# Loading q and k two rows at a time, turned by DMA transposes and sorted by copies, in a fused attention and feed-forward kernel

## The chip, the cores and the metric

The kernel runs on one core of a Trainium2 chip. The metric is the time of one execution on the device in microseconds (us). The kernel before takes 318.61 us, the median of 3 runs (318.08 to 319.79).

## The reference

What is computed is an attention over a sliding window of 64 positions, whose output feeds a two-layer network with the activation h cos h:

```python
batch, n_heads, seq, head_dim = (8, 8, 576, 64)
scores = scale * np.matmul(q, k.transpose(0, 1, 3, 2))
mask = (rel >= 0) & (rel < window)            # rel = pos[:, None] - pos[None, :], window = 64
scores = np.where(mask, scores, -1000000000.0)
attn = np.exp(scores - np.max(scores, axis=-1, keepdims=True))
attn = attn / (np.sum(attn, axis=-1, keepdims=True) + 1e-09)
x = np.matmul(attn, v)                        # to rows (batch, seq) x columns (head, dim): 4608 x 512
h = x @ w_in                                  # w_in: 512 x 2048
out = (h * np.cos(h)) @ w_out                 # w_out: 2048 x 512
```

All inputs and the output are float32. The kernel computes in bf16 with float32 sums.

## The kernel before

**The row tiles.** The outer loop runs over 9 tiles of 512 rows (`mt`, 0 to 8). Each has two halves. In the first, for each of 16 blocks `ff` of 128 hidden columns, four matmuls of 512 columns (`h_ps`, line 341) are summed in PSUM; ScalarE (ACT) takes the sine of h + pi/2 (line 486) and VectorE (DVE) multiplies it with h to `gT` (line 489). In the second half 64 matmuls (`out_ps`, line 501) multiply `gT` with w_out. The h_ps blocks use five PSUM banks in turn (`H_BANKS`), so that the matmuls of a block need the bank that an earlier block's gT has freed.

**The attention lies between them.** While tile `mt` is worked on, the scores of batch `mt` + 1 are computed in between, for the outputs that tile `mt` + 1 needs. Heads go in pairs (`PAIRS` = 4): a pair's 2 x 64 dimensions fill the 128 partitions. Keys must lie as kT (dimensions of a pair on partitions, positions along the free axis). For batches 2 to 7 queries lie in `qB` (`qblocks`), one block for each 64 positions, where a pair's two heads stand in a diagonal of two 64 x 64 squares with zeros beside them, so that one matmul (line 248) computes both heads. A group of three or four such units goes through scores on TensorE (PE), mask and maximum on DVE (line 268), exp on ACT (line 279), the inverse of the sum on DVE (line 286), the multiplication to `w` on GpSimd (POOL, line 293), and a DMA transpose from the SP queue to `wT` (line 305). The products with v (`values`, line 320) close the tile.

**How q and k of batches 2 to 7 come.** `load_chunk` (line 146) loads 96 positions of all 8 heads, with a cast to bf16, from POOL's queue: 6 chunks each of q and k, 64 elements to a row of a head. Queries are turned by PE: `transposed` (line 180) makes six transposes of 96 x 128 for a pair into one PSUM tile, and `put_block` copies the two heads on DVE into their places in `qB` (line 113, the shared copy helper). Keys of batch 2 go the same way (`tr_k`, `put_k`, the copy on ACT), those of batches 3 to 7 by `turn_k` (line 213): six DMA transposes a batch from SP, each of four 128-column blocks, straight into kT. Batches 0 and 1 are loaded in another form (`load_heads`, nine consecutive rows to a partition) and turned by PE, line 177.

**The order.** Every engine works through its own queue in order; the kernel writes that order by hand. Tile 0 follows the list `FIRST`. After that `at(time, fn, ...)` puts steps on a plan, and `pump(time)` issues those that are due after each block of matmuls. A tile is 32 units of this plan, of which the first 16 follow the blocks `ff` and the others four out_ps matmuls each; the times are no microseconds, they only fix the places in the queues. Scores begin at unit 14.6 of a tile (line 382). The last group of a batch has its inverse, its w and its wT at the tile's end (line 386). DMA loads are issued by POOL, DMA transposes and stores of the output by SP, so a waiting instruction there holds up the transfers behind it. Loads of v (line 152, five a batch) come at the head of a tile; `spread_v` copies half of v on POOL (line 113) before the scores.

Of the kernel before, what the change touches and what calls it, by code (L numbers as in the profile page):

```python
# [15 lines left out]
BF16 = mybir.dt.bfloat16  # L16
# [7 lines left out]
NU = 9  # L24
NC, NP = 6, 96
# [33 lines left out]
def kernel(  # L59
# [28 lines left out]
    qtiles = [const.tile([128, S], BF16, name=f"qT{i}") for i in range(2 * PAIRS)]  # L88
    qblocks = [const.tile([128, NU, 2, 64], BF16, name=f"qB{i}") for i in range(2 * PAIRS)]
# [42 lines left out]
    def rows_tile(name):  # L132
        return ld.tile([128, NC * H * D], BF16, tag=name, name=name)
# [36 lines left out]
    def transposed(name, b, p):  # L170
        t_ps = ps_t.tile([128, S], BF16, tag="t", name=f"t{name}_ps")
        of = st[name, b]
        if b < 2:
            for c in range(RC):
                for h in range(2):
                    d = slice(64 * h, 64 * h + 64)
                    nc.tensor.transpose(t_ps[d, 64 * c:64 * c + 64], of[d, p, 64 * c:64 * c + 64], ident[d, d])  # L177
        else:
            for c in range(NC):
                nc.tensor.transpose(t_ps[:, NP * c:NP * c + NP], of[:, c, 128 * p:128 * p + 128], ident[:NP, :NP])  # L180
        return t_ps


    def in_order(t_ps, to, b):
        return (t_ps.rearrange("d (c p) -> d p c", c=RC), to.rearrange("d (p c) -> d p c", c=RC)) if b < 2 else (t_ps, to)
# [4 lines left out]
    def put_q(b, p, engine=None):  # L190
        of, to = in_order(st.pop(("tq", b, p)), qtiles[b * PAIRS + p], b)
        if b:
            copy(engine, to, of)
        elif engine == "a":
            nc.scalar.mul(to, of, scale)
        else:
            nc.vector.tensor_scalar(to, of, scale, None, ALU.mult)

    def put_block(b, p, h):
        d = slice(64 * h, 64 * h + 64)  # L200
        copy("d", qblocks[(b % 2) * PAIRS + p][d, :, h], st["tq", b, p][d].rearrange("d (j t) -> d j t", j=NU))
# [10 lines left out]
    def turn_k(b, c):  # L212
        nc.sync.dma_start(out=k_tile(b)[:, :, c * NP:c * NP + NP], in_=st["k", b][:, c], transpose=True)

    def put_k(b, p, engine="a"):
        kt = k_tile(b)[:, p]
        of, to = in_order(st.pop(("tk", b, p)), kt, b)
        copy(engine, to, of)
# [13 lines left out]
    def g_scores(n, which):  # L232
# [8 lines left out]
        for u, (b, p, j) in enumerate(units):  # L241
# [5 lines left out]
            if b > 1:  # L247
                nc.tensor.matmul(out=s_ps[:, u].rearrange("p (a t) -> p a t", a=2),  # L248
                                 lhsT=qblocks[(b % 2) * PAIRS + p][:, j].rearrange("d h t -> d (h t)"), rhs=rhs,
                                 start=True, stop=True, skip_group_check=True)  # L250
                continue
            for h in range(2):
                d = slice(64 * h, 64 * h + 64)
                nc.tensor.matmul(out=s_ps[d, u].rearrange("p (a t) -> p a t", a=2),  # L254
                                 lhsT=qtiles[b * PAIRS + p][d, 64 * j:64 * j + 64], rhs=rhs[d], start=n >= n_first,
                                 stop=n >= n_first or u == len(units) - 1, skip_group_check=True)
# [91 lines left out]
    def clear(i):  # L348
        nc.gpsimd.memset(qblocks[i].rearrange("d j h t -> d (j h t)"), 0.0)
# [18 lines left out]
    def at(time, fn, *args):  # L368
        plan.append((time, len(plan), fn, args))
# [25 lines left out]
    for b in range(1, B):  # L395
        t0 = T * (b - 1)
        for p in range(PAIRS):
            t_q = 7 + 1.8 * p if b == 1 else t0 + 1 + 2.5 * p if b == 2 else t0 + 1 + 3.5 * p
            steps = (((0, tr_q), (0.01, tr_k), (0.02, put_q), (0.03, put_k)) if b == 1 else
                     ((0, tr_q), (0.02, put_block, 0), (0.5, put_block, 1)) +  # L400
                     (((9.5 - 0.8 * p, tr_k), (9.51 - 0.8 * p, put_k)) if b == 2 else ()))
            for lag, fn, *args in steps:
                at(t_q + lag, fn, b, p, *args)
        if b > 1:
            for c in range(NC):
# [10 lines left out]
    for p in range(PAIRS):  # L416
        at(T + 3 + 4 * p, clear, PAIRS + p)
# [13 lines left out]
    for t in qblocks[:PAIRS]:  # L431
        nc.vector.memset(t.rearrange("d j h t -> d (j h t)"), 0.0)
# [108 lines left out]
```

## Time and profile before

| | |
|---|---|
| median of 3 runs | 318.61 us (318.08 to 319.79) |
| span of the profiled execution | 316.6 us |
| instructions in the profile | 7858 |
| busy: PE, DVE, ACT, POOL | 300.1, 227.8, 238.3, 196.6 us |
| DMA | 39.91 MB in 150697 packets, 139392 of them under 512 B |
| queue of POOL's loads (q0) | 99824 packets, 18.36 MB |
| queue of SP's transposes and stores (q1) | 50688 packets, 20.85 MB |

The runs were timed without the profiler; the profiled execution's own time is known by its span, from its first instruction to its last, and the median lies 2.0 us above it for what surrounds the span. PE stands for TensorE's matmuls and PEld for its weight loads, which overlap them. In a list of instructions "out<-in" names the tiles, then come the shapes (partitions x elements), the number of instructions and their time; a bracket at the end gives the idle time of the engine before and what ended it. L113 is the helper `copy`, so copies are told apart by their tiles. SPq and POOLq are the queues in which DMAs are issued: the time of such a row is that of issuing, not of the transfer. In a table of windows each engine's entry is its busy time and, in brackets, its number of instructions; the last three numbers are the granted clock of TensorE, the share of the DMA engines and GB/s.

The stages' length hardly varies in the middle: the windows 160 to 192, 192 to 224 and 224 to 256 us have PE busy for 31.76 us each, with a granted clock of 1.00.

### The profile page before, as it was taken

To read this page: it belongs to the slowest core of one execution; us is meant where nothing else is said; L and a number is where in the kernel's file an instruction comes from. 1 tells how busy PE (TensorE), PEld (TensorE's weight loads), DVE (VectorE), ACT (ScalarE), POOL (GpSimd) and SP (SyncE) were. 2 spreads that over 40 slices of the span, in tenths; PEclk is the share of its full clock that TensorE was granted. 3 is DMA by queue.
4 is the path that set the end of the run, shared out by engine and by line. 5 is a ranking of instruction groups with operands and counts; after the bars stand their busy time and mean duration, and the time that the engine had idled before them with its cause. 6 is when DMAs were issued, how large, how long until landed. Compare 5 with 4: busy or idle time off the path is not lost.

```text
span 316.6 us, 7858 instructions
## 1 busy us (share of the span) xinstructions
PE 300.1 (95%) x2580; PEld 157.5 (50%) x2620; DVE 227.8 (72%) x871; ACT 238.3 (75%) x789; POOL 196.6 (62%) x228
## 2 busy tenths in 40 slices
PE   3678999999999999999999999999999999999995
PEld 2544545555555544545554555555555554454443
DVE  5976778689767977697859885997599758335801
ACT  3978689868998689869986998699868996115600
POOL 8896156799969767897788878986832630000000
PEclk9979999999999999999999999999999999999999
DMA  6999996699959994899989997999692442011011
GB/s 97 170 211 207 207 148 90 70 194 162 160 92 98 151 228 85 88 153 231 124 91 140 230 123 83 158 218 127 77 179 92 81 105 100 2 66 69 0 66 66
DMA packets 150697, 39.91 MB, mean 126 GB/s; under 512 B 139392, under 2 KB 146176, under 8 KB 150656
## 3 DMA queue, kind: packets, MB, share of 16 engines
q0 software_dynamic: 99824, 18.36, 75.7%
q1 hardware_dynamic: 50688, 20.85, 32.5%
q8 instruction: 20, 0.33, 0.4%
q14 instruction: 21, 0.17, 0.2%
q10 hardware_dynamic: 144, 0.20, 0.2%
HBM read 36.70 MB, written 9.44 MB: 146 GB/s over the span
## 4 chain that ended last, share of the span: by engine, by line
PE 81%; DVE 6%; ACT 5%; POOL 3%; issue 2%; DMA 2%; POOLq 0%
PE h_ps L341 35%; PE out_ps L501 34%; ACT e L279 3%; PE s_ps L248 3%; DVE gT L489 3%; PE o_ps L320 3%; DMA k<-in_k_dram 2%; PE tq_ps L180 2%; PE s_ps L254 1%; POOL w L293 1%; PE out_ps L356 1%; DVE qB L113 1%; PE tw_ps L302 1%; POOL v L113 1%; PE tk_ps L177 1%
## 5 line engine op out<-in xcount | busy, mean ns | idle before, releaser
L341 PE MATMUL h_ps<-xT,w_in 128*128 128x512 bf16 x556 | 130.5, 379 | 2.9 <-ACT xT L113 1.0
L501 PE MATMUL out_ps<-w_out,gT 128*128 128x512 bf16 x543 | 130.9, 379 | 1.2 <-issue 0.5
L486 ACT ACTIVATE sin<-h_ps 128x512 f32<-128x512 f32 x144 | 83.6, 598 | 39.2 <-PE h_ps L341 36.2
L489 DVE TENSOR_TENSOR gT<-h_ps,sin 128x512 bf16<-128x512 f32 x144 | 92.2, 685 | 27.1 <-ACT sin L486 26.2
L279 ACT ACTIVATE e<-s,negm 128x128 f32<-128x128 f32 x256 | 98.7, 388 | 1.0 <-DVE negm L268 0.9
L293 POOL TENSOR_TENSOR w<-e,rden 128x512 bf16<-128x512 f32 (+1 forms) x78 | 74.0, 958 | 35.6 <-DVE rden L286 29.1
L341 PEld LDWEIGHTS <-w_in 128*128 128x128 bf16 x576 | 54.3, 98 | 60.7 <-issue 2.4
L501 PEld LDWEIGHTS <-gT 128*128 128x128 bf16 x560 | 51.5, 98 | 49.7
L268 DVE CUSTOM_DVE_ANT_0 s<-s_ps,mask 128x128 f32<-128x128 f32 x256 | 58.2, 285 | 1.9 <-PE s_ps L254 1.6
L279 ACT ACTIVATION_READ_ACCUMULATOR e<-s,negm 128x1 f32 x256 | 48.1, 188 | 0.0
L146 POOL DMA_DIRECT2D q<-in_q_dram x36 | 28.9, 804 | 12.3 <-PE h_ps L341 4.7
L152 POOL DMA_DIRECT2D v<-in_v_dram x40 | 34.1, 874 | 3.0 <-DMA k<-in_k_dram 2.0
L146 POOL DMA_DIRECT2D k<-in_k_dram x36 | 29.0, 806 | 3.2 <-DMA k<-in_k_dram 2.4
L113 ACT COPY out_sb<-out_ps 128x512 f32<-128x512 f32 (+1 forms) x18 | 10.1, 563 | 25.7 <-PE out_ps L501 20.2
L286 DVE RECIPROCAL rden<-den 128x4 f32<-128x4 f32 (+1 forms) x80 | 13.9, 173 | 20.9 <-ACT e L279 18.3
L113 DVE CAST xT<-o_ps 128x512 bf16<-128x512 f32 x27 | 17.5, 678 | 9.9 <-PE o_ps L320 9.9
L113 DVE COPY out_sb<-out_ps 128x512 f32<-128x512 f32 x18 | 12.4, 689 | 16.6 <-PE out_ps L501 12.6
L248 PEld LDWEIGHTS <-qB 128*128 128x128 bf16 x216 | 17.0, 98 | 14.6 <-DVE negm L268 0.6
L113 POOL COPY v<-v 64x2048 bf16<-64x2048 bf16 (+1 forms) x11 | 18.7, 1701 | 5.4 <-DMA v<-in_v_dram 5.0
L248 PE MATMUL s_ps<-kT,qB 128*128 128x128 bf16 x216 | 21.9, 219 | 0.2 <-DVE negm L268 0.2
L113 DVE COPY qB<-tq_ps 64x576 bf16<-64x576 bf16 x48 | 21.6, 450 | 0.3
L268 DVE DVE_READ_ACCUMULATOR2_ANT negm<- 128x1 f32 x256 | 21.3, 83 | 0.0
(57 smaller groups left out, 187.5 us busy)
## 6 DMA issues: line engine op xcount, KB each, us to landing
out_dram<-out_sb SPq DMA_DIRECT2D x16, 512.0 KB, 6.8
v<-in_v_dram POOLq DMA_DIRECT2D x32, 128.0 KB, 6.2
q<-in_q_dram POOLq DMA_DIRECT2D x36, 96.0 KB, 7.1
k<-in_k_dram POOLq DMA_DIRECT2D x36, 96.0 KB, 7.5
w_out<-in_moe_w_out_dram POOLq DMA_DIRECT2D x2, 1024.0 KB, 16.4
w_in<-in_moe_w_in_dram POOLq DMA_DIRECT2D x2, 768.0 KB, 11.8
wT<-w SPq DMA_TRANSPOSE x66, 2.9
out_dram<-out_sb SPq DMA_DIRECT2D x3, 256.0 KB, 2.0
```

What stands on the lines that cost most here:

```text
L113: {"a": nc.scalar.copy, "p": nc.gpsimd.tensor_copy}.get(engine, nc.vector.tensor_copy)(out, in_)
L146: nc.gpsimd.dma_start(out=st[name, b][:, c].rearrange("p (h d) -> p h d", h=H), in_=src.rearrange("h p d -> p h d"))
L152: nc.gpsimd.dma_start(out=vt.rearrange("p (h d) -> p h d", h=H), in_=v[b, :, c * 128:c * 128 + n, :].rearrange("h p d -> p h d"))
L248: nc.tensor.matmul(out=s_ps[:, u].rearrange("p (a t) -> p a t", a=2), lhsT=qblocks[(b % 2) * PAIRS + p][:, j].rearrange("d h t -> d (h t)" ...
L268: nc.vector.tensor_tensor_reduce(out=s[:, u], in0=s_ps[:, u], in1=mask[:, 2 - j % 2 if j else 0], scale=-scale if b else -1.0, scalar=BIG, ...
L279: nc.scalar.activation(e[:, u], s[:, u], AF.Exp, bias=negm[:, u:u + 1], scale=1.0 if n < n_first else -1.0, accum_out=den[:, u:u + 1])
L286: nc.vector.reciprocal(out=rden[:, 0:len(groups[n])], in_=den[:, 0:len(groups[n])])
L293: (nc.gpsimd if engine == "p" else nc.vector).tensor_tensor(out=w[:, 0:u], in0=e[:, 0:u], op=ALU.mult, in1=rden[:, 0:u].unsqueeze(2).to_br ...
L341: nc.tensor.matmul(out=st["h", ff], lhsT=w_in_sb[:, ks, ff * 128:ff * 128 + 128], rhs=st["xT", mt][:, ks], start=start, stop=stop)
L486: nc.scalar.activation(sin, h_ps, AF.Sin, bias=math.pi / 2.0)
L489: nc.vector.tensor_tensor(out=gt[:, e], in0=h_ps, in1=sin, op=ALU.mult)
L501: nc.tensor.matmul(out=o_ps[e], lhsT=gT[ff // 2][:, ff % 2, ms * 128:ms * 128 + 128], rhs=w_out_sb[:, ff], start=ff == 0, stop=ff == n_ff - 1)
```

## The change

It concerns q and k of batches 2 to 7.

- `load_rows` takes the place of `load_chunk`. A partition gets two consecutive rows of a head (128 elements), and a batch's q or k comes in two DMAs of four heads each (96 x 12 x 128), in place of six: four loads a batch from POOL, not twelve.
- `turn` sends each half through one DMA transpose from SP (12 blocks of 96 x 128). Its result X has the even rows' dimensions on partitions 0 to 63 and the odd rows' on 64 to 127. There are four such DMA transposes a batch, placed at units 0.3 to 2.3 of the tile in which the batch's scores are computed; the PE transposes of q and of k of batch 2, `put_block` and the former `turn_k` go.
- `sort_rows` copies X into kT and into qB, every second position at a time: four copies for k and four for q, each of 64 partitions x 1152 elements, two of each four on DVE and two on POOL, at units 6.2 to 11.7 of the same tile. Both halves of X must have landed for each.
- X shares its two buffers with the tiles that hold the queries of batches 0 and 1. `qB` becomes one tile for each parity of batches. `clear` still zeroes the second one's four parts on POOL in tile 1.

The program's order after the change has on PE 168 transposes fewer with their weight loads. On SP a tile (2 to 6) has: the last wT of the old one, Xk, a store, Xk, a store, Xq, Xq, then the new wT. On POOL: the last w, five loads of v, a sort of k, a load of k, a sort of k, two loads (k, q), a sort of q, a load of q, a sort of q, then `spread_v` and the w. On DVE the sorts of k stand before and after the ninth gT of the tile (ff = 8), those of q before and after the thirteenth (ff = 12). The first score matmul of a tile waits for DVE and POOL. In tile 1 the four X transposes come one after the other, and the memsets of `clear` stand between POOL's loads and sorts.

```diff
-NC, NP = 6, 96
+NG, NP = 3, 96
...
-    qtiles = [const.tile([128, S], BF16, name=f"qT{i}") for i in range(2 * PAIRS)]
-    qblocks = [const.tile([128, NU, 2, 64], BF16, name=f"qB{i}") for i in range(2 * PAIRS)]
+    qblocks = [const.tile([128, PAIRS, NU, 2, 64], BF16, name=f"qB{i}") for i in range(2)]
...
-    def load_chunk(name, b, c):
+    def load_rows(name, b, half):
         if (name, b) not in st:
-            st[name, b] = rows_tile(name)[0:NP].rearrange("p (c x) -> p c x", c=NC)
-        src = {"q": q, "k": k}[name][b, :, c * NP:c * NP + NP]
-        nc.gpsimd.dma_start(out=st[name, b][:, c].rearrange("p (h d) -> p h d", h=H),
-                            in_=src.rearrange("h p d -> p h d"))
+            st[name, b] = rows_tile(name)[0:NP].rearrange("p (m x) -> p m x", x=2 * D)
+        m = slice(half * H // 2 * NG, (half + 1) * H // 2 * NG)
+        src = {"q": q, "k": k}[name][b].rearrange("h (g p c) d -> p (h g) (c d)", g=NG, c=2)
+        nc.gpsimd.dma_start(out=st[name, b][:, m], in_=src[:, m])
...
-    def put_block(b, p, h):
-        d = slice(64 * h, 64 * h + 64)
-        copy("d", qblocks[(b % 2) * PAIRS + p][d, :, h], st["tq", b, p][d].rearrange("d (j t) -> d j t", j=NU))
...
-    def turn_k(b, c):
-        nc.sync.dma_start(out=k_tile(b)[:, :, c * NP:c * NP + NP], in_=st["k", b][:, c], transpose=True)
+    def turn(name, b, half):
+        if ("X" + name, b) not in st:
+            st["X" + name, b] = att.tile([128, H * NG, NP], BF16, tag="X", name="X" + name, bufs=2)
+        m = slice(half * H // 2 * NG, (half + 1) * H // 2 * NG)
+        nc.sync.dma_start(out=st["X" + name, b][:, m], in_=st[name, b][:, m].rearrange("p m x -> p (m x)"), transpose=True)
+
+    def sort_rows(name, b, c, h):
+        of = st["X" + name, b][64 * c:64 * c + 64].rearrange("d (a h g) p -> d a h (g p)", a=PAIRS, h=2)[:, :, h]
+        d = slice(64 * h, 64 * h + 64)
+        if name == "k":
+            to = k_tile(b)[d, :, c::2]
+        else:
+            to, of = qblocks[b % 2][d, :, :, h, c::2], of.rearrange("d a (j p) -> d a j p", j=NU)
+        copy("p" if c == h else "d", to, of)
...
-            for c in range(NC):
-                for i, name in enumerate(("q", "k")):
-                    at(t0 - T + (5.6 + 1.6 * c + 0.8 * i if b > 2 else 27.5 + 0.9 * c if i else 4 + 0.5 * c), load_chunk, name, b, c)
-            for c in range(NC if b > 2 else 0):
-                at(t0 - 5.5 + c, turn_k, b, c)
+            for i, name in enumerate(("k", "q")):
+                for half in range(2):
+                    at((4 if b == 2 else t0 - T + 7) + 3 * i + 1.5 * half, load_rows, name, b, half)
+                    at(t0 + 0.3 + 1.5 * i + 0.5 * half, turn, name, b, half)
+                    for c in range(2):
+                        at(t0 + 6.2 + 4 * i + c + 0.5 * half, sort_rows, name, b, c, c if half else 1 - c)
```

More of the change, by code (lines that the diff above doesn't have):

```diff
@@ L132, in rows_tile @@
     def rows_tile(name):
-        return ld.tile([128, NC * H * D], BF16, tag=name, name=name)
+        return ld.tile([128, NG * 2 * H * D], BF16, tag=name, name=name)
     def load_heads(name, b, p0=0, n=PAIRS):
@@ L172, in transposed, with in_order, q_tile @@
         of = st[name, b]
-        if b < 2:
-            for c in range(RC):
-                for h in range(2):
-                    d = slice(64 * h, 64 * h + 64)
-                    nc.tensor.transpose(t_ps[d, 64 * c:64 * c + 64], of[d, p, 64 * c:64 * c + 64], ident[d, d])
-        else:
-            for c in range(NC):
-                nc.tensor.transpose(t_ps[:, NP * c:NP * c + NP], of[:, c, 128 * p:128 * p + 128], ident[:NP, :NP])
-        return t_ps
-    def in_order(t_ps, to, b):
-        return (t_ps.rearrange("d (c p) -> d p c", c=RC), to.rearrange("d (p c) -> d p c", c=RC)) if b < 2 else (t_ps, to)
+        for c in range(RC):
+            for h in range(2):
+                d = slice(64 * h, 64 * h + 64)
+                nc.tensor.transpose(t_ps[d, 64 * c:64 * c + 64], of[d, p, 64 * c:64 * c + 64], ident[d, d])
+        return t_ps
+    def in_order(t_ps, to):
+        return t_ps.rearrange("d (c p) -> d p c", c=RC), to.rearrange("d (p c) -> d p c", c=RC)
+    def q_tile(b):
+        if ("qT", b) not in st:
+            st["qT", b] = att.tile([128, PAIRS, S], BF16, tag="X", name="qT", bufs=2)
+        return st["qT", b]
     def tr_q(b, p):
@@ L396 @@
         t0 = T * (b - 1)
[L397 to L405, printed above, removed]
-                for i, name in enumerate(("q", "k")):
-                    at(t0 - T + (5.6 + 1.6 * c + 0.8 * i if b > 2 else 27.5 + 0.9 * c if i else 4 + 0.5 * c), load_chunk, name, b, c)
-            for c in range(NC if b > 2 else 0):
-                at(t0 - 5.5 + c, turn_k, b, c)
+        if b == 1:
+            for p in range(PAIRS):
+                for lag, fn in ((0, tr_q), (0.01, tr_k), (0.02, put_q), (0.03, put_k)):
+                    at(7 + 1.8 * p + lag, fn, b, p)
+        else:
+            for i, name in enumerate(("k", "q")):
[4 more added lines that the diff above has]
+                        at(t0 + 6.2 + 4 * i + c + 0.5 * half, sort_rows, name, b, c, c if half else 1 - c)
             for c in range(5):
@@ L416 @@
     for p in range(PAIRS):
-        at(T + 3 + 4 * p, clear, PAIRS + p)
+        at(T + 3 + 4 * p, clear, p)
     for mt in range(1, n_mt):
@@ L430 @@
     exp_table()
-    for t in qblocks[:PAIRS]:
-        nc.vector.memset(t.rearrange("d j h t -> d (j h t)"), 0.0)
+    for p in range(PAIRS):
+        nc.vector.memset(qblocks[0][:, p].rearrange("d j h t -> d (j h t)"), 0.0)
     make_identity(nc, ident)
```

13 lines of the change are left out of this document (6 added, 7 removed).

## The prediction

> **What bounds the kernel now.** I read the page's busy shares and slices first, then the chain of work that ended last, then the table of windows, then the timeline of one middle stage, engine by engine. From the page:
>
> ```profile
> PE 300.1 (95%) x2580; PEld 157.5 (50%) x2620; DVE 227.8 (72%) x871; ACT 238.3 (75%) x789; POOL 196.6 (62%) x228
> PE   3678999999999999999999999999999999999995
> PE 81%; DVE 6%; ACT 5%; POOL 3%; issue 2%; DMA 2%; POOLq 0%
> ```
>
> TensorE is full from the fourth slice on, and the chain runs through it for 81% of the span. A stage is one row tile (`mt`). From the first h_ps matmul of stage 6, at 192.62 us, to that of stage 7, at 224.62, is 32.0 us; the window beside it shows what is idle:
>
> ```profile
> 192.00:224.00 32.00, 31.76 (x260) 16.66 (x260) 25.75 (x112) 27.38 (x96) 26.28 (x29) 1.00 1.46 145
> ```
>
> The busy times are PE 31.76, PEld 16.66, DVE 25.75, ACT 27.38, POOL 26.28 of 32. So what leaves PE is gained in full, and every wait that PE is given is paid in full. I call the stage's first h_ps matmul S and count from it.
>
> **What the change takes off PE.** The timeline of PE in that stage:
>
> ```profile
> 204.62 0.42 PE L180 MATMUL tq_ps<-ident,q 96*128 96x96 bf16 x6
> 204.88 2.76 PE L341 MATMUL h_ps<-xT,w_in 128*128 128x512 bf16 x12
> 207.47 0.39 PE L248 MATMUL s_ps<-kT,qB 128*128 128x128 bf16 x4
> ```
>
> Six transposes push the next matmul back by 204.88 - 204.62 = 0.26 us. There are 168 of them (144 of q, 24 of k of batch 2), 28 groups: 28 x 0.26 = 7.2 us, four groups (1.03 us) in each of stages 2 to 6 and eight in stage 1. The first score matmul stands at 207.47 = S+14.85; without the four groups PE would reach it at S+13.8. From it to the next S are 17.15 us, which do not change.
>
> **What it adds, and where it waits.** In the changed kernel's order the first score matmul of stages 1 to 6 waits for DVE and POOL, for all eight sort copies. On SP the four X transposes of a stage (12 blocks each; k, k, q, q, a store behind each k) stand behind the last wT transpose of the old stage, which waits for POOL's last w:
>
> ```profile
> 224.72 1.04 POOL L293 TENSOR_TENSOR w<-e,rden 128x512 bf16<-128x512 f32 x1 [0.95 <-DVE rden L286]
> 225.71 4.27 POOL L152 DMA_DIRECT2D v<-in_v_dram  x5
> ```
>
> and SP's queue in the same place, where the last wT of the stage still stands behind kT transposes (it went out at 232.79):
>
> ```profile
> 222.97 3.19 SPq L213 DMA_TRANSPOSE kT<-k  x2
> 226.27 1.20 SPq L305 DMA_TRANSPOSE wT<-w  x1
> ...
> 232.79 1.21 SPq L305 DMA_TRANSPOSE wT<-w  x1
> ```
>
> The last w ends at 225.76 = S+1.1. The last wT is then issued to S+2.4 (1.2 us each), Xk0 to S+3.7, a store (two took 1.03) to S+4.3, Xk1 from S+4.4. The 1.2 us are the same for 3 and for 4 blocks; a 12-block one is not in the trace: 1.2 us if the price is one of the instruction, 3.6 if of the blocks. I take 1.2, since 3 and 4 blocks do not differ, and keep 3.6 for the range.
>
> When Xk has **landed** is a matter of the DMA engines. From S+1.1 on POOL issues five loads of v (576 rows x 8 heads, 4608 packets of 128 B). Four windows of the DMA view, packets of each queue: 195.1 to 202.1 (v and q/k loads beside transposes), 217 to 218 (transposes alone), 73 to 78 (loads alone), 209 to 212 (stores, mostly):
>
> ```profile
> q0 software_dynamic: 5051, 0.64, 142.2%
> q1 hardware_dynamic: 1280, 0.30, 33.9%
> ...
> q1 hardware_dynamic: 1011, 0.25, 135.1%
> ...
> q0 software_dynamic: 6105, 0.77, 241.2%
> ...
> q1 hardware_dynamic: 457, 0.90, 90.0%
> ```
>
> Alone, transposes pass 1011 packets/us, loads 6105/5 = 1221, stores 457/3 = 152. Side by side loads pass 722/us and transposes 183: v goes nearly first. An X half is 12 x 96 = 1152 packets (1011 packets for 0.25 MB are 256 B each, one row of a block; a kT of 4 blocks has 384). Work until both halves of Xk lie in SBUF: v 4608/1221 = 3.8, wT and Xk 2816/1011 = 2.8, the store between them 256/152 = 1.7; 8.3 us from S+2.5, so **S+10.8, say S+11**. The early bound: Xk1 issued at S+4.4, the shortest landing of a transpose 2.4 us, 768 packets more than that one 0.8: S+7.6.
>
> Behind this wait POOL has in order: sort, k load, sort, k load, q load, sort, q load, sort. Rows for these:
>
> ```profile
> L113 POOL COPY v<-v 64x2048 bf16<-64x2048 bf16 x6 | 11.3, 1891 | 0.4
> L113 POOL COPY v<-v 64x1536 bf16<-64x1536 bf16 x5 | 7.4, 1472 | 5.0 <-DMA v<-in_v_dram 5.0
> ```
>
> and, from the timeline near the start, the only large DVE copy between SBUF tiles, beside POOL:
>
> ```profile
> 18.75 2.22 POOL L293 TENSOR_TENSOR w<-e,rden 128x512 bf16<-128x512 f32 x2
> 19.09 1.23 DVE L113 COPY v<-v 64x1536 bf16<-64x1536 bf16 x1
> ```
>
> The copies differ by 0.419 us for 512 elements, so a sort of 1152 costs 1.16 us. It writes every second element, which no row shows; the bounds are 1.16 and twice that, and I take 1.16 as the copy is the nearest row. A load of 768 packets is issued in 0.80 us, one of 1024 in 0.87; 1152 packets give 0.91. Four of each: 4.6 + 3.6 = 8.3 us (rounded up), none of it beside other work of POOL. Xq is needed at S+11 + 5.1 = S+16 and lands about then (a store 1.7, 2304 packets 2.3, the two k loads 0.9 each between), so I add no wait for it.
>
> DVE has four sorts too. In the timeline above the first of the two w ends at 19.79, the copy at 20.33, and the second w took 1.22 instead of 1.04. So the two engines get in each other's way; a copy of 1536 took between 0.54 and 1.23 us. I put a sort at 0.8 (bounds 0.4, the 0.54 scaled, and 1.5, twice the 0.747 of a 576-element strided copy from PSUM) and **one collision of 0.7 us a stage** on POOL's chain. DVE's own chain (two sorts and a gT of 0.6 after Xq's S+16: S+18.2) ends before POOL's and costs nothing more. The eight qB copies that go (8 x 0.45 = 3.6 us) lay under PE, as do the 4 kT copies of ACT (0.63 each) in stage 1. POOL's 12 loads become 4, SP's 16 transposes 14, and 9216 load packets a batch 4608; all were under PE. The k loads of batch 2 leave the tail of stage 0, where PE is idle 0.4 us in 21: I take 0.
>
> The rule that speaks against the sorts is in the Trainium skill, SBUF — State Buffer, section Who interferes with whom: a VectorE copy in a two-port mode and a GpSimd instruction exclude each other for a whole instruction. The 1.23 us copy agrees. By it each of DVE's four sorts could hold POOL for 0.8 us, 2.5 us a stage above my 0.7, an estimate of 15 us in all.
>
> **Sum.** Last sort at S+11 + 8.3 + 0.7 = S+20.0, PE at the scores 0.15 later: S+20.15 instead of S+14.85, so each stage grows by 5.3 us (a stall of 6.3 less the 1.03 gained). Stage 1 gains 2.06 but POOL has two 1.15 us memsets more in its chain; I take the same. 6 x 5.3 = 31.8; the span 316.6 becomes 348.4. The median of the runs is 2.0 us above the profiled span: **350.4 us**.
>
> **Rivals.** (a) *Faster, 311 us*: all is hidden and 7.2 us are won. That needs Xk landed 8.3 us before S+13.8, at S+5.5; Xk1 is only issued at S+4.4, and no transpose landed under 2.4 us. Only sorts of half my price on POOL move the point to S+7.8, so that S+7.6 would do: 0.05; no change 0.03. (b) *Early landing*: the transposes get in ahead of v, landing at S+7.6 to S+9.5: last sort S+16 to S+18.5, 1.1 to 3.7 us a stage: 325 to 341 us. For it: v is issued over 4.3 us. Against: 722 to 183 packets. 0.24. (c) *The issue or the sort is dearer*: 3.6 us a transpose puts Xq at S+20.6, the last sort at S+23.8, 9 us a stage: 373; sorts of 2.3 us give the same. 0.14. (d) *The clock*: from 8 to 16 us PE was busy 66%, and the granted clock was 0.62 over the window 16 to 20.5, which is 3.4 us at half. PE would be mostly idle from S+11.3 (h_ps has five banks, and the sixth gT behind the wait comes late) to S+20; 3.4 us at half clock cost 1.7 a stage, 10 us on top: 360. 0.16. The Trainium skill says so too (TensorE: Matmul & The Clock Gate, section Part 1: an idle window of some 3.4 us halves the clock); the trace's 0.62 agrees. My forecast itself, 343 to 358: 0.38. That the transposes do not leave PE is excluded: the order has 168 matmuls fewer.
>
> **Chances and range.** Slower by over 0.5% (what a measurement of this kernel can tell from no change) 0.92, within 0.03, faster 0.05. The range reaches from (b)'s low end to a little over (c)'s: 325 to 376.
>
> **What would show it.** Right: the chain passes through POOL's sorts in stages 1 to 6; PE waits at the first score for POOL, some 5 to 7 us; the X transposes land 6 us or more after issue; stages of about 37 us. Wrong: a first score at S+14, or the X transposes landed before S+7; then POOL's chain is done in time. If SP shows 3.6 us a transpose, (c); if the granted clock falls below 1.00 in stages 1 to 6, (d).

## The result and the profile after

The changed kernel takes **386.59 us**, the median of 4 runs (386.30 to 387.42), against 318.54 us (318.08 to 319.79) for the kernel before, which has one run more here than in the table ahead of the prediction: 1.214 times as long, 95% interval 1.211 to 1.217. Forecast were 350.4 us, with a range of 325 to 376. So the direction was right and the size was not: the loss is 68 us where 32 were expected. From the page of the changed kernel, busy time, PE's slices, the granted clock by slice, and the chain that ended last:

```profile
PE 315.9 (82%) x2413; PEld 156.4 (41%) x2452; DVE 236.8 (61%) x847; ACT 238.3 (62%) x785; POOL 208.0 (54%) x204
PE   3789999647996599846995499944997699999996
PEclk9989999977998699986999689986999589999999
PE 61%; POOL 14%; DMA 14%; DVE 4%; issue 3%; ACT 2%; SPq 1%; POOLq 0%; DVEq 0%
```

TensorE was full from the fourth slice on; now it falls to 4 to 6 tenths once in each stage, and its clock falls with it. It has 167 instructions fewer in the records and is yet busy 15.8 us longer, since part of its matmuls run at half the clock. The shares of POOL and DMA in the chain have grown from 3% and 2% to 14% each. The waits of the changed kernel (us in total, times, the longest):

```profile
POOL kT L112 <- DMA Xk<-k: 49.5, 6, 9.7
...
DVE kT L112 <- DMA Xk<-k: 31.4, 6, 6.6
...
PE s_ps L255 <- POOL qB L112: 26.2, 5, 6.3
PE h_ps L348 <- DVE gT L494: 26.1, 10, 5.2
...
PE s_ps L255 <- DVE qB L112: 1.3, 1, 1.3
```

POOL and VectorE both stand at their first sort for Xk, once in each of the six stages. TensorE stands twice, first at an h_ps whose bank VectorE has not freed, then at the first score. There it waits for POOL in stages 1 to 5; in stage 6 VectorE's last sort ends last, and the wait for it is 1.3 us. In stage 4 (S = 196.23) SP issues Xk, a store, Xk:

```profile
198.70 2.02 SPq L211 DMA_TRANSPOSE Xk<-k  x1
200.82 1.14 SPq L371 DMA_DIRECT2D out_dram<-out_sb  x1
202.06 2.80 SPq L211 DMA_TRANSPOSE Xk<-k  x1
```

and the second half lands at 209.83, S+13.6. POOL's chain behind it begins so:

```profile
209.95 2.10 POOL L112 COPY kT<-Xk 64x1152 bf16<-64x1152 bf16 x1 [8.36 <-DMA Xk<-k]
211.96 1.25 POOL L146 DMA_DIRECT2D k<-in_k_dram  x1
213.25 1.48 POOL L112 COPY kT<-Xk 64x1152 bf16<-64x1152 bf16 x1
```

The first sort and the load behind it run beside copies of VectorE, as do the second load of k (1.32 us) and the first sort of q (1.89); with none beside them a sort takes 1.45 to 1.48 us and a load 0.87. The chain ends at 221.04, 11.2 us after the landing. TensorE in the same stage:

```profile
211.50 0.81 PE L348 MATMUL h_ps<-xT,w_in 128*128 128x512 bf16 x2 [3.89 <-DVE gT L494]
...
221.09 0.61 PE L255 MATMUL s_ps<-kT,qB 128*128 128x128 bf16 x4 [4.91 <-POOL qB L112]
```

The first score stands at 221.09 = S+24.9, forecast S+20.15, before S+14.85. And the rest of the stage, which was to stay at 17.15 us, is 19.25 long (a row of the windows; the number before the last two is the granted clock):

```profile
221.09:240.34 19.25, 19.12 (x163) 10.17 (x166) 11.39 (x86) 15.62 (x75) 11.81 (x11) 0.89 0.40 64
```

TensorE is busy for all of it, at a mean clock of 0.89: the record has it at half from 218.56 to 225.39 us, 4.3 us of it behind the first score, which is 2.1 us of work lost. The six stages, from S to the next S in us (profiled executions):

| stage | 1 | 2 | 3 | 4 | 5 | 6 | sum |
|---|---|---|---|---|---|---|---|
| before | 33.77 | 32.45 | 32.55 | 32.03 | 31.99 | 31.99 | 194.8 |
| changed | 45.74 | 43.48 | 45.16 | 44.11 | 44.82 | 40.60 | 263.9 |

The sums differ by 69.1, the spans (385.6 and 316.6) by 69.0: the whole loss lies in the six stages. Stage 6 is the shortest; it issues no loads of k and q, since there is no batch 8.

### The profile page after: what moved, and what is told of

Read it like the earlier page. It is cut to its first block, busy times and chain, and to the rows that moved or that the text cites. A ratio compares the mean times of both kernels' runs of the same rounds, so it can differ in the third digit from the quotient of the medians.

```text
span 385.6 us, 7439 instructions
## 1 busy us (share of the span) xinstructions
PE 315.9 (82%) x2413; PEld 156.4 (41%) x2452; DVE 236.8 (61%) x847; ACT 238.3 (62%) x785; POOL 208.0 (54%) x204
## 4 chain that ended last, share of the span: by engine, by line
PE 61%; POOL 14%; DMA 14%; DVE 4%; issue 3%; ACT 2%; SPq 1%; POOLq 0%; DVEq 0%
PE out_ps L506 34%; PE h_ps L348 17%; DMA Xk<-k 13%; POOL qB L112 4%; PE s_ps L255 4%; POOL kT L112 3%; POOL k L146 3%; PE o_ps L327 2%; POOL q L146 2%; ACT sin L491 2%; DMA k<-in_k_dram 1%; PE s_ps L261 1%; PE out_ps L363 1%; DVE gT L494 1%; DVE qB L112 1%
## 5 line engine op out<-in xcount | busy, mean ns | idle before, releaser
L348 PE MATMUL h_ps<-xT,w_in 128*128 128x512 bf16 x557 | 136.8, 397 | 29.0 <-DVE gT L494 26.1
L506 PE MATMUL out_ps<-w_out,gT 128*128 128x512 bf16 x543 | 140.5, 401 | 1.4 <-issue 0.7
L494 DVE TENSOR_TENSOR gT<-h_ps,sin 128x512 bf16<-128x512 f32 x144 | 93.3, 686 | 28.6 <-ACT sin L491 27.9
L348 PEld LDWEIGHTS <-w_in 128*128 128x128 bf16 x576 | 57.7, 101 | 100.9 <-issue 41.8
L275 DVE CUSTOM_DVE_ANT_0 s<-s_ps,mask 128x128 f32<-128x128 f32 x256 | 59.1, 285 | 38.6 <-PE s_ps L255 36.5
L506 PEld LDWEIGHTS <-gT 128*128 128x128 bf16 x560 | 54.2, 102 | 55.7 <-issue 10.0
L112 POOL COPY kT<-Xk 64x1152 bf16<-64x1152 bf16 x12 | 21.9, 1821 | 49.8 <-DMA Xk<-k 49.5
L255 PE MATMUL s_ps<-kT,qB 128*128 128x128 bf16 x216 | 23.9, 234 | 27.5 <-POOL qB L112 26.2
L255 PEld LDWEIGHTS <-qB 128*128 128x128 bf16 x216 | 18.1, 105 | 45.7 <-POOL qB L112 31.0
L112 DVE COPY kT<-Xk 64x1152 bf16<-64x1152 bf16 x12 | 12.2, 1016 | 31.6 <-DMA Xk<-k 31.4
L112 ACT COPY out_sb<-out_ps 128x512 f32<-128x512 f32 (+1 forms) x18 | 10.3, 571 | 27.6 <-PE out_ps L506 22.2
L112 DVE COPY out_sb<-out_ps 128x512 f32<-128x512 f32 x18 | 12.4, 691 | 14.1 <-PE out_ps L506 13.7
L112 POOL COPY qB<-Xq 64x1152 bf16<-64x1152 bf16 x12 | 19.6, 1637 | 0.5
L112 POOL COPY v<-v 64x2048 bf16<-64x2048 bf16 (+1 forms) x11 | 19.2, 1750 | 0.8 <-DMA v<-in_v_dram 0.3
L146 POOL DMA_DIRECT2D k<-in_k_dram x12 | 14.5, 1209 | 8.6 <-PE tk_ps L175 5.2
```

What stands on the lines that cost most here:

```text
L112: {"a": nc.scalar.copy, "p": nc.gpsimd.tensor_copy}.get(engine, nc.vector.tensor_copy)(out, in_)
L146: nc.gpsimd.dma_start(out=st[name, b][:, m], in_=src[:, m])
L275: nc.vector.tensor_tensor_reduce(out=s[:, u], in0=s_ps[:, u], in1=mask[:, 2 - j % 2 if j else 0], scale=-scale if b else -1.0, scalar=BIG, ...
L348: nc.tensor.matmul(out=st["h", ff], lhsT=w_in_sb[:, ks, ff * 128:ff * 128 + 128], rhs=st["xT", mt][:, ks], start=start, stop=stop)
L494: nc.vector.tensor_tensor(out=gt[:, e], in0=h_ps, in1=sin, op=ALU.mult)
L506: nc.tensor.matmul(out=o_ps[e], lhsT=gT[ff // 2][:, ff % 2, ms * 128:ms * 128 + 128], rhs=w_out_sb[:, ff], start=ff == 0, stop=ff == n_ff - 1)
```

## The experiments

Theory: the turns of k stand on SP behind wT and move beside v; Xk lands late; POOL's chain of sorts and loads starts there and ends at the first score; the standstill of TensorE halves its clock, which makes the rest of the stage longer too. Rivals: the banks of h_ps (VectorE's wait) are what holds TensorE; SP's issues, not the DMA engines, set the landing; the sorts are dear by themselves; the clock falls for another reason. Six kernels each take one part away. The ratios are taken against runs of the kernel before that were made beside each kernel (medians of 317.55 to 318.54). Means over stages 2 to 5 of the profiled executions, in us from S (the last column: from the first score to the next S):

| kernel | time, median | to before (95%) | Xk landed | first score | rest |
|---|---|---|---|---|---|
| before | 318.54 | 1 | | 15.0 | 17.2 |
| changed | 386.59 | 1.214 (1.211 to 1.217) | 13.9 | 25.2 | 19.2 |
| e1, loads behind the sorts | 367.62 | 1.153 (1.146 to 1.159) | 13.5 | 22.0 | 18.9 |
| e2, turns a stage early | 341.88 | 1.074 (1.068 to 1.080) | before S | 16.7 | 17.6 |
| e3, no loads of v | 366.44 | 1.152 (1.148 to 1.156) | 9.7 | 21.0 | 19.4 |
| e4, TensorE kept busy | 375.98 | 1.183 (1.179 to 1.187) | 13.4 | 24.7 | 17.2 |
| e5, stores behind the turns | 381.21 | 1.198 (1.195 to 1.202) | 12.4 | 23.7 | 19.3 |
| e6, ScalarE sorts for VectorE | 368.23 | 1.154 (1.149 to 1.159) | 13.9 | 23.3 | 17.2 |

**e1: loads behind the sorts.**

```diff
-at((4 if b == 2 else t0 - T + 7) + 3 * i + 1.5 * half, load_rows, name, b, half)
+at(4 + 3 * i + 1.5 * half if b == 2 else t0 - T + 12 + 0.6 * i + 0.3 * half, load_rows, name, b, half)
```

> The row loads of batches 3 to 7 are issued on POOL behind the sorts instead of between them. Theory (the first score waits for POOL's chain of sorts with the loads in it): the four loads cost 1.25 + 1.32 + 0.87 + 0.87 = 4.3 us of that chain in stages 1 to 5, and stage 6, which has none, is 3.8 us shorter than the mean of the others; so 5 stages by about 4 = 20 us less, near 366 us, with stages 1 to 5 at 40 to 41 as stage 6. Rival 1 (TensorE is held up by the banks of h_ps, which VectorE frees only when its own wait for Xk is over): VectorE's wait is the same, no change, 386. Rival 2 (only the landing of Xk at S+13.6 counts, and POOL catches up behind it): no change, 386.

19.0 us less, where the theory said about 20. The timeline of POOL, stage 4 (S = 186.48):

```profile
199.31 4.08 POOL L112 COPY kT<-Xk 64x1152 bf16<-64x1152 bf16 x2 [7.46 <-DMA Xk<-k]
203.44 3.43 POOL L112 COPY qB<-Xq 64x1152 bf16<-64x1152 bf16 x2
```

Four sorts in one piece, 7.6 us instead of 11.2, and stages 2 to 5 are nearly as short as stage 6 (40.1 to 41.7; stage 6, where nothing was moved, 40.5, in the changed kernel 40.6). Both rivals called for 386 and fall: what stands in POOL's chain is paid at the first score. But POOL is no longer what ends last: in all six stages the first score now waits for VectorE's last sort (12.1 us in all), which in stage 4 ends at 207.52, 0.65 us after POOL's.

**e2: turns a stage early.**

```diff
-at(t0 + 0.3 + 1.5 * i + 0.5 * half, turn, name, b, half)
+at(t0 + (0.3 if b == 2 else 13 - T) + 1.5 * i + 0.5 * half, turn, name, b, half)
```

> The turns of batches 3 to 7 are issued on SP late in the stage before, ahead of the turns of w; batch 2's stay, so that stage 1 is as in the changed kernel. Theory (Xk lands at S+13.6 because it is issued behind wT and moves beside v, and POOL's chain of 11.1 us starts there): with Xk there before S, POOL's chain starts behind the loads of v, at about S+5.5, and ends at S+16.6, or with fewer collisions earlier; stages 2 to 6 fall from 44 to about 34, 5 by 10 less = 336, and down to 328 if the chain gets shorter. Rival 1 (the sorts' own price, with the exclusion of VectorE and POOL, is what counts): the first score stays behind S+20, 360 or more. Rival 2 (the early turns hold up wT on SP, and with it the first layer's start): S itself is late, with TensorE waiting for wT, 350 or more.

44.7 us less, with stage 1, left as it was, at 46.1 (45.7): the late landing is the largest single cause. Stages 3 to 6 have the first score at S+16.7 to S+18.1, the rest at 17.14 and the clock at 1.00. Rivals 1 and 2 fall as the main cause, but a part of the first is there: in stages 2 to 6 the first score waits for VectorE's last sort, 10.3 us in five waits. The last sorts of both engines in stage 5 (S = 210.73):

```profile
224.93 1.87 POOL L112 COPY qB<-Xq 64x1152 bf16<-64x1152 bf16 x1
226.21 1.25 DVE L112 COPY qB<-Xq 64x1152 bf16<-64x1152 bf16 x1
```

POOL's chain ends at S+16.1, VectorE's at S+16.7. In stage 6, with no loads, POOL has done its sorts by S+11.9, and VectorE's run at S+8.5, S+11.3, S+14.5 and S+17.2 between the gT.

**e3: no loads of v** (`for c in range(5 if b == 2 else 0)` at `load_v`).

> Leaves out the loads of v of batches 3 to 7, so that their outputs are formed with an old v. Theory (Xk's landing is set by the DMA engines that it shares with v's 4608 packets): Xk lands in stages 2 to 6 at S+9.5 to S+11 instead of S+13.6, and each of the 5 stages gets 2.6 to 4 us shorter: 366 to 374. Rival (the landing is set by SP's issues, 2.0 and 2.8 us each, or by the transposes' own rate): it stays at S+13 or later, 383 to 387.

Xk lands 4.2 us earlier, the stages get 4 us shorter. SP's second turn of k in stage 4:

```profile
194.30 1.64 SPq L211 DMA_TRANSPOSE Xk<-k  x1
```

This one is issued in 1.64 us and not in 2.80, the first in 1.32 and not in 2.02. So the long issues are no price of 12 blocks: with v in flight the same issues take longer. The rival's S+13 falls, but 9.7 us remain without v. A part of that is the transposes' own rate: from 192 to 193 and from 193 to 194 us, with no load beside them, their queue passed 514 and 494 packets, half of the 1011 per us that the forecast took.

**e4: TensorE kept busy.**

```diff
+    def busy(n):
+        o = ps_t.tile([128, MT], F32, tag="t", name="busy_ps")
+        for _ in range(n):
+            nc.tensor.matmul(out=o, lhsT=w_out_sb[:, 0, 0:128], rhs=w_out_sb[:, 0], start=True, stop=True)
...
+    for t in range(1, B - 1):
+        at(T * t + Q - 1.45, busy, 20)
...
+            if ff == 13 and 1 <= mt <= 6:
+                busy(16)
```

> Adds matmuls that nothing reads, 16 ahead of the 14th step of the first layer and 20 ahead of the first score of stages 1 to 6, where TensorE stands still. Theory (the half clock of 6.8 us in each stage, two stretches behind the two standstills, follows from the standstills): the granted clock stays at 1.00 there, the part from the first score to the next S falls from 19.25 to about 17.2, 6 by 2.1 = 12.5 us less, near 374. If the stretches come for another reason (the load on the chip): they stay, and the time is 386 or some us more for the added matmuls.

10.6 us less with 216 matmuls more. Stage 4, from the first score to the next S:

```profile
213.81:230.96 17.15, 17.02 (x162) 9.37 (x165) 11.39 (x86) 15.63 (x75) 11.82 (x11) 1.00 0.44 72
```

17.15 us at a clock of 1.00, as in all of stages 1 to 6. So the half clock of the changed kernel followed from the standstills, and not from the load on the chip.

**e5: stores behind the turns** (`at(base + T + 7 + ms0 / 2, store, ...)` for all tiles).

> The two stores of each output tile are issued on SP behind the turns of k and q (from the second stage on) instead of between them. If SP's issues set the landing of Xk: the store of 1.14 us in front of the second turn goes, Xk lands at S+12.4 instead of S+13.6, each of 6 stages is 1.2 to 1.5 us shorter, 377 to 380. Rival (the landing is set by what the DMA engines can move beside v, whatever the order on SP): it stays at S+13.6, 385 to 387.

5.4 us less: Xk lands 1.5 us earlier. The time is a little above the band, between the two predictions and nearer to the first; the store in front of the second turn costs about what it was put at.

**e6: ScalarE sorts for VectorE** (`"d"` becomes `"a"` in the copy of `sort_rows`).

> VectorE's four sorts of each batch are done by ScalarE; POOL's four stay. If the exclusion of VectorE and POOL is what makes POOL's chain 11.1 us instead of 9.0: POOL's sorts of 2.10 and 1.89 us fall to 1.45 each and the loads of 1.25 and 1.32 to 0.87, 1.9 us less in stages 1 to 5 and some 1.1 in stage 6, near 376. Rival 1 (the sorts and loads are dear by themselves): POOL's durations stay, 386. Rival 2 (the price moves: ScalarE, which runs sin, waits for Xk in VectorE's place and holds up h_ps as long): POOL's chain is shorter, but the first score is set by ScalarE, 380 to 390.

18.4 us less, more than expected. POOL and TensorE in stage 4 (S = 186.98):

```profile
200.90 1.45 POOL L112 COPY kT<-Xk 64x1152 bf16<-64x1152 bf16 x1 [8.55 <-DMA Xk<-k]
202.27 0.88 POOL L146 DMA_DIRECT2D k<-in_k_dram  x1
```

```profile
203.71 4.85 PE L348 MATMUL h_ps<-xT,w_in 128*128 128x512 bf16 x12 [5.35 <-DVE gT L494]
210.15 0.40 PE L255 MATMUL s_ps<-kT,qB 128*128 128x128 bf16 x4 [1.59 <-POOL qB L112]
```

Without a VectorE copy beside it each sort of POOL takes 1.45 to 1.48 us and each issue of a load 0.87 to 0.88; the chain is 9.3 us long, not 11.2. That is the expected 1.9 us. The rest is the clock: the half clock lies at 200.92 to 207.75, where TensorE has h_ps to do and would wait for POOL anyway. The wait at the first score is 1.6 us, not 4.9, no half clock follows it, and the stretch behind the first score is back at 17.16. Rival 2 is there (TensorE's long wait is now the one for gT), but POOL still ends last in stages 1 to 5.

**Versions that mend the order.** With the causes known, ten kernels try to keep the gain of TensorE without the waits. All turn batches 3 to 7 a stage early, e16 only 4 to 7. Stage lengths of the profiled executions in us:

| kernel | time, median | to before (95%) | stage 0 | 1 | 2 | 3 to 5, mean | 6 |
|---|---|---|---|---|---|---|---|
| before | 318.54 | 1 | 39.6 | 33.8 | 32.4 | 32.2 | 32.0 |
| e7, batch 2 early too; DVE's sorts in gaps | 330.16 | 1.038 (1.033 to 1.042) | 40.0 | 38.1 | 34.5 | 34.3 | 32.6 |
| e8, DVE's k sorts a stage before | 325.64 | 1.023 (1.021 to 1.026) | 39.4 | 39.2 | 34.2 | 32.8 | 31.0 |
| e9, e8 with rows a stage earlier | 320.26 | 1.006 (1.004 to 1.008) | 45.8 | 34.7 | 31.6 | 31.4 | 31.0 |
| e10, e7 with rows a stage earlier | 323.41 | 1.014 (1.011 to 1.018) | 43.6 | 37.0 | 33.4 | 31.7 | 31.7 |
| e11, e9, batch 3's rows in stage 1 | 325.15 | 1.022 (1.019 to 1.026) | 40.2 | 43.6 | 31.9 | 31.6 | 31.0 |
| e12, e11, batch 4's rows later | 324.95 | 1.020 (1.016 to 1.024) | 40.2 | 43.5 | 33.7 | 31.6 | 31.0 |
| e13, rows, then sorts | 319.53 | 1.005 (1.003 to 1.007) | 39.8 | 36.5 | 33.7 | 31.6 | 31.0 |
| e14, e13, all k sorts on DVE | 320.05 | 1.007 (1.004 to 1.009) | 39.9 | 36.9 | 34.0 | 31.5 | 31.0 |
| e15, e13, batch 2 by TensorE | 323.93 | 1.018 (1.016 to 1.020) | 40.4 | 39.5 | 34.0 | 31.9 | 31.0 |
| e16, e13, batches 2, 3 as before | 322.59 | 1.016 (1.013 to 1.019) | 40.1 | 33.8 | 38.5 | 32.4 | 31.0 |

In e7 to e12 POOL's sorts stand right behind the loads of v and the loads of rows behind the sorts, but for batch 3's rows in e11 and e12; from e13 on the loads of rows stand between v and the sorts. The lines, cut to their part for batches 3 to 7:

```diff
+at(t0 + 5.55 + 0.5 * i + 0.1 * c, sort_rows, name, b, c, c)
+at(t0 + ((-0.45, -0.44), (3.2, 7.2))[i][c], sort_rows, name, b, c, 1 - c)
+at(t0 + ((-4.5, -3), (-0.45, -0.44))[i][c], sort_rows, name, b, c, 1 - c)
+at(t0 - 2 * T + (15 if b == 3 else 12) + 0.6 * i + 0.3 * half, load_rows, name, b, half)
+at(t0 - T + 5.5 + 0.02 * i + 0.01 * half, load_rows, name, b, half)
+at(t0 - T + 9 + 0.2 * i + 0.1 * half, turn, name, b, half)
```

The first line is POOL's sorts, the next two VectorE's in e7 and e10 and in the others; then the row loads of e9 and e10 and those of e13 to e16 (two lines), and the turns from e9 on; the turns of batch 2 stand at units 18 and 28.6 of tile 0 (not in e15 and e16). In e13 VectorE's third sort of k stands at unit -6.5.

> All turns a stage early (batch 2's too, late in stage 0), the row loads on POOL behind its sorts, POOL's sorts right behind the loads of v, VectorE's sorts of k in its idle time ahead of the first gT and those of q behind the fifth and the ninth, the memsets of qB behind the loads. Theory (the change itself frees TensorE of 1.03 us a stage, and what made it slower is only the wait for Xk and POOL's chain): POOL's sorts end at S+11.5, ahead of TensorE's own S+13.8, the clock stays at 1.00 and six stages take 31.0 to 31.5 us: 311 to 314, faster than both kernels. Rival (VectorE becomes the bound: 16 gT by 0.69 + xT 1.25 + four sorts of 0.8 to 1.25 = 15.5 to 17.3 us ahead of the first score): first score at S+15.5 to S+17, stages 33 to 34, 322 to 330.

> As the kernel with all turns early, but VectorE's sorts of k (batches 3 to 7) run in the softmax stretch of the stage before, and those of q in the idle time ahead of the first gT. Theory: VectorE has only gT and POOL only its own sorts ahead of the first score, S+13.8; stages of 31.0, 310 to 313. Rival (the sorts there hold up the softmax chain that ends each stage, since VectorE's reciprocals feed POOL's w): the next S is later by up to their 1.6 us, 313 to 322.

Both miss. e7 lies just above the band of its rival (322 to 330), and its stage 6 shows the rival's price: a first score at S+15.5 and 32.6 us. In e8 POOL is in time, but the stages with loads are up to 8 us too long, while stage 6, which has none, is at 30.97. A large part of it is SP's queue, as in e8's stage 2 (S = 100.60), first a row of POOL, then SP:

```profile
120.50 0.82 POOL L300 TENSOR_TENSOR w<-e,rden 128x384 bf16<-128x384 f32 x1 [4.47 <-issue]
```

```profile
115.12 5.02 SPq L211 DMA_TRANSPOSE Xk<-k  x2
120.31 3.00 SPq L211 DMA_TRANSPOSE Xq<-q  x2
123.43 12.87 SPq L312 DMA_TRANSPOSE wT<-w  x9
```

A w is ready at 121.3, but the turns, which wait for rows issued behind the sorts, stand in front of its transpose until 123.4; nine of those take 12.9 us, so that SP cannot catch up, and TensorE waits for wT at the stages' ends, 9.3 us in all, up to 2.4 at a time. With the longest of these goes a half clock (0.53 in the mean from 97.5 to 104.7 us). What the rest of e8's loss consists of is left open. What I had called rival 2 in e2 (turns hold up wT) is real.

> As the kernel with VectorE's sorts of k in the stage before, but the rows of k and q are loaded one stage earlier still (behind the sorts of the stage three before their own, batch 3's late in stage 0), so that the turns are issued on SP at about S+9 to S+15 and not at S+14 to S+22, where the ten turns of w queue up behind them. Theory (what is left in stages 1 to 5 of that kernel is SP's queue: TensorE waits 9.3 us for wT in front of S, and the second part takes 17.8 to 22.5 us instead of 17.15): all second parts at 17.15, stages 2 to 6 at 31.0, stage 1 at about 33, 311 to 313, faster than both kernels. Rival (VectorE's sorts in the softmax stretch are what lengthens it): second parts stay at 17.8 to 19.9, 317 to 322.

> The same earlier loads and turns, with VectorE's sorts of k in its gap ahead of the first gT and those of q behind the fifth and the ninth. Theory: the second parts are at 17.15 as well; the first score is at S+14.0 to S+15.5, by VectorE's 15.5 to 16 us of work with up to three h_ps in hand; stages 31.2 to 32.6, 312 to 320. If VectorE's sorts in the first part cost nothing, it equals the other kernel.

With rows a stage earlier the turns are out of the way, and e9's stages 2 to 6 are at 31.0 to 31.7, close to the theory's 31.0. e10 shows VectorE's price: 0.8 us a stage with first scores at S+14.6 instead of S+13.8. But e9's stage 0 grew by 6 us and e10's by 4, which the expectations had not seen, and so both totals miss (311 to 313 and 312 to 320 were expected).

> As the kernel with the rows a stage earlier, but batch 3's rows are loaded at the head of stage 1, ahead of the loads of v, and not late in stage 0. Theory (that kernel lost in stage 0 what it gained in stages 2 to 6: there the rows of batch 3 moved beside the last turns of w, which landed 8 us after their issue instead of 2.4, and S of stage 1 came at 67.3 us instead of 61.4): stage 0 is back at 39.4 to 40.2, stage 1 at 34 to 35.5, stages 2 to 6 stay at 31.0 to 31.6: 313 to 316, faster than both kernels. Rival (the loss of stage 0 comes from batch 2's early turns): stage 0 stays at 45, 319 to 321.

> The same, and in stage 1 batch 4's rows are loaded behind the four memsets of qB, some 4 us later, so that the turns of batch 3 have the DMA engines for themselves. Theory: stage 1 loses its wait for wT, 32.5 to 33.5 us instead of 34.7, in all 312 to 315. Rival (POOL's first w in stage 1 is then 1 to 2 us late, and the softmax chain carries it to S): no gain over the other, 313 to 317.

Stage 0 is back, as expected, and its rival falls; stage 1 is 9 us longer than in e9, so that both miss. Rows of two batches, v, four turns and ten wT meet in one stage, and the last two loads of rows land 20 and 22 us after their issue.

> All turns early; on POOL the loads of v, then the rows for the stage after next, then the sorts, and of those one less (VectorE takes a third sort of k, in the softmax stretch of the stage before, batches 3 to 7). So each stage loads one batch's rows and no more, and its turns are issued before the turns of w begin. If the 61 us belong to the order alone: POOL 1.1 + 4.3 + 3.6 + 3 by 1.48 = S+13.4, ahead of TensorE's S+13.8; stage 0 at 39.4 to 40.2, stage 1 at 34 to 36, stages 2 to 6 at 31.0 to 31.7: 312 to 316, faster than both kernels. If a part of them belongs to what the DMA engines have to move (rows, turns and v in one stage): the turns of w land late again, second parts of 18 to 20, 319 to 326.

> The same with all four sorts of k of batches 3 to 7 on VectorE in the softmax stretch, two on POOL. POOL ends at S+12. If POOL's end were still what holds the first score of the other kernel, this one has it at S+13.8 and is up to 1 us a stage faster; if VectorE's sorts lengthen the softmax chain, its second parts are longer by up to 0.8 us each and it is the slower one. 311 to 318.

e13 is the best of the versions, 1.005 (1.003 to 1.007), still not faster than before; 312 to 316 us were expected, so it misses too. The rival's second parts of 18 to 20 us are there, but in stages 1 and 2 alone (19.7 and 18.2). Its windows of stages 4 and 6:

```profile
163.28:194.85 31.57, 31.10 (x229) 15.52 (x228) 27.37 (x109) 27.38 (x95) 26.79 (x25) 1.00 1.20 165
...
226.48:257.44 30.96, 30.94 (x232) 15.61 (x229) 25.04 (x107) 26.74 (x94) 22.18 (x20) 1.00 0.67 103
```

The stages from 3 on are 0.4 to 1.0 us shorter than before, at full clock; stages 1 and 2 lose 4 us. In e14 the first scores of stages 3 to 5 come 0.5 us earlier and the rest of these stages is 0.3 to 0.4 us longer: no gain, and again above the band.

> As the kernel with rows, then sorts, but batch 2 goes the way of the kernel before (its q and k loaded by 96 rows, turned by TensorE, put by VectorE and ScalarE); batches 3 to 7 are turned by DMA. If what is left of the loss lies in the two stages in which the order starts up (36.5 and 33.7 us there against 33.8 and 32.45 before, while stages 3 to 6 are at 31.0 to 31.6 against 32.0 to 32.55): stage 0 at 39.6, stage 1 at 33.8 to 35, stage 2 at 32.0 to 32.5, stages 3 to 5 at 31.6, stage 6 at 31.0, 314.5 to 316.5, faster than both kernels by about 0.9% of before. If instead batch 3's rows and turns in stage 1 hold up wT there whatever batch 2 does: stage 1 stays at 36 to 37, 317 to 319, no gain.

> Batches 2 and 3 go the way of the kernel before (loads by rows of 96, turned by TensorE, batch 3's k by six DMA turns); batches 4 to 7 are turned by DMA in the order rows, then sorts, so that the first rows and turns of that kind come in stage 2. If the loss that is left lies where the turns of q and k meet the start of the pipeline (stage 1, where the rows land at S+14 to S+25 and the turns push wT to S+27): stages 0 to 2 as before, 39.6, 33.8 and 32.5 to 33.0, then 31.6, 31.6, 31.6 and 31.0: about 316, 0.7 to 1% faster than before. If every first stage of the turns pays for them: stage 2 is 34 to 37, and the time 317 to 320.

Both miss, by more than their rivals allowed, but on the rivals' side: the loss moves with the stage in which the early turns begin (stage 1 in e15, stage 2 in e16), where they wait for rows that arrive beside the last transfers of the old form. In e16 the first wT goes out at S+27.3, 7.5 us after its w, in e13's stage 2 at S+21.7. The stage of the start is 5.7 us longer than before in e15, 6.0 in e16; stage 1 of e13 is 2.7 us longer. Which transfer there would have to move is left open.

## Why the prediction was wrong

Mechanism and place were right: the chain runs through Xk's landing and POOL's sorts, and in stages 1 to 5 TensorE waits for POOL at the first score (5.2 us in the mean, forecast 5 to 7). That this number fits is partly luck: the forecast had one standstill of 6.3 us, and in stage 4 TensorE stood for 8.8 in two, 3.9 of them at an h_ps. In stage 6 VectorE's chain ends last, which the forecast had ended before POOL's. The terms of the sum were too small. For stages 2 to 5, of which each is 12.1 us longer than before and 5.3 were forecast:

- **"Xk landed S+11".** It landed at S+13.9: 2.9 us. Of the parts, v (put at 3.8) cost 4.2 by e3 and the store (1.7) 1.5 by e5; what failed is the rest, wT and the two halves of Xk, put at 2.8 us from S+2.5: without v, but with the store, they were not there before S+9.7 in the mean. Less the store's 1.5 that is 5.7 us from S+2.5, 2.9 more than forecast, if the parts simply add. Two things of it are seen in e3's stage 4: the first half of Xk went at half the rate that I had taken from a window of wT, and the sum counted packets alone, with nothing for the time from issue to landing, 3.3 us for the first half and 4.4 for the second. In e3's stages 2 and 3 the first turn was also issued only at S+3.5 and S+3.1. The 1.2 us an issue that I took were nearly right without v (1.3 and 1.6); beside v, in stages 2 to 6, they were 1.4 to 2.0 for the first half and 2.5 to 3.3 for the second, and a line that I showed (two turns of k in 3.19) had warned of it. Rival (c), 3.6 us a turn, falls, as do its sorts of 2.3 us. Rival (b), early landing, falls with the landing. The shortest landing before was 2.3 us, not 2.4; no term hangs on it.
- **"4 sorts and 4 loads 8.3, one collision 0.7".** 11.2 instead of 9.0. A sort costs 1.45 us and not 1.16 (4 x 0.29 = 1.2): with its every second element it takes as long as v's copy of 1536 elements (1.47), not of 1152. The collisions cost 1.9 and not 0.7, by e6 against the changed kernel. The loads were right (0.87 for 0.91) where nothing collided.
- **"17.15 us, which do not change".** 19.2. This is rival (d): 2.0 us a stage by e4 (1.7 forecast), 10.6 us in all (10). I gave it a chance of 0.16 as a case of its own, where it followed from my own forecast, in which TensorE stood still for 6 us.
- 2.9 + 2.2 + 2.0 = 7.1 for the missing 6.8 a stage; the first score of before, which stood at S+15.0 in these stages in the mean and not at 14.85, makes up most of the difference.
- **"6 x 5.3".** Stage 6 issues no loads, so its chain should have been 3.6 us shorter by my own prices; it is, with 8.6 us lost in place of 12.1.
- **The 1.03 us that TensorE gains** are right, but only seen once nothing waits: stage 6 of e8, e9, e13 and e14 takes 30.95 to 30.97 (31.99 before), with its first score at S+13.8, the forecast point. They were never lost; they lay under the wait.

The range failed because its rivals were kept apart. A dearer chain, a later landing and a slower clock can all hold at once, and here each makes the next one likelier: the sum of (d) and of the collisions at the higher price, 10 + 15 us on 350, is 375, the end of the range, and the later landing comes on top.

The collisions lie about halfway between my 0.7 us and the rule that I had weighed. The Trainium skill (SBUF — State Buffer, section Who interferes with whom) has the second of the two engines block for a whole instruction. The estimate by it was 2.5 us above my 0.7, measured were 1.2 above it. The same section says that a DMA which a VectorE operation stalls is one whose descriptors GpSimd writes, and that GpSimd was starved of the time to write them. The trace agrees: 1.25 and 1.32 us for an issue of 0.87.

## What to carry to other kernels

When a step leaves the bounding engine for a chain over a queue, a DMA and two other engines, price the chain from what it shares at that moment: what stands before it in the queue, what moves beside it, what the waiting engine still has to issue. Rivals that lengthen the same wait are added, not chosen between, and the half clock that followed TensorE's long waits here (2.8 to 6.3 us, two a stage) belongs in the sum. Moving work a stage earlier mends the steady state, but the queue that takes it (SP with its ten wT a stage) and the first stage in the new rhythm have to be priced as well.

## What the runs showed of the hardware

- The half clock of TensorE came in stretches of 3.41, 6.83 and 10.24 us. In the changed kernel it cost 2.0 us a stage; in e6's stage 4 a standstill of 5.4 us brought 6.83 us of it, which cost nothing behind the first score, as the stretch lay where TensorE waited for POOL anyway.
- How long TensorE has to stand for it is not settled by these runs: a wait of 1.9 us in e2's stage 2 had 3.41 us at half behind it (124.32 to 127.73), one of 3.1 us in e4's stage 1 had none (clock 1.00 from 85 to 96).
- An issue on SP is not a fixed price. The two turns of k, 12 blocks each, took 1.3 and 1.6 to 1.7 us without v and 1.4 to 2.0 and 2.5 to 3.3 beside it (stages 2 to 6 of e3 and of the changed kernel).
- A copy of 64 x 1152 bf16 into every second element took 0.80 us on VectorE alone and 1.0 to 2.5 beside work of POOL; on POOL 1.45 to 1.48 alone and, in the changed kernel, 1.9 to 2.1 beside VectorE; on ScalarE 1.46 to 1.48.
